# Block products for the second token pair, late gate tiles and one-column modulation products in an adaLN attention and gMLP block

## The chip, the cores and the metric

One core of a Trainium2 chip runs the whole kernel. The time is the device time of one launch in microseconds (us), the median of several runs of the same program. A profiled execution has its own time; its span, from the first to the last instruction that the profile shows, is a little shorter.

## What is computed

One batch of 2048 tokens of width 512 goes through two residual blocks that are modulated by a condition c: linear attention with 32 heads, then a gated MLP whose gate mixes along the tokens.

```python
mod = (silu(c) @ w_mod).reshape(1, 6, 1, -1)
sa, ca, ga, sb, cb, gb = (mod[:, i] for i in range(6))
h = layernorm(x) * (1 + ca) + sa
x = x + ga * linear_attention(h, wqkv, wo)      # phi = elu + 1, 32 heads of 16
h = layernorm(x) * (1 + cb) + sb
z = gelu(h @ w_in)                              # [2048, 1376]
z1, z2 = z[..., :688], layernorm(z[..., 688:])
g = w_sp @ z2 + b_sp[:, None]                   # [2048, 2048] x [2048, 688]
out = x + gb * ((z1 * g) @ w_out)
```

All of it is float32.

## The kernel before, in words

**Numbers.** TensorE takes operands of type float32r here, so every factor is kept in two parts, a high part (`x_hi`, made by ACT as a copy into float32r) and a low part (`x - x_hi`, made by DVE or POOL), and every product is three matmuls: high by high, high by low, low by high. "A low part" of a tile is thus one subtraction of its size on DVE or POOL, behind a copy on ACT.

**Phases.** The tokens are 16 tiles of 128. Phase 1 (to some 200 us) reads the modulation, folds `1 + ca` into the attention's weights, normalizes, and forms keys, values and their sums. At the start `col_mm` (L189) multiplies blocks of `w_mod` by a repeated column of silu(c); the result is a 128 by 4 by 128 PSUM tile, all columns of a block alike, which `mean_col` (L324) copies as it stands and `col_end` (L204) reads one column of. Dummy products (`du`, on the tile `warm`) fill PE's first microseconds.

Phase 2 goes tile by tile through the attention's output, `h2`, its transposed parts `ht2`, and `z_mm` (L652): 24 matmuls of 128x344 each for z1 (`z0` in the order) and z2 (`z1` in the order). `z1_out` puts gelu(z1) into DRAM (`z1d`). `z2_out` makes `zz`, which is normalized (`zb` is the shift), parked in DRAM (`zd`), and split into `z2` (`zh` high part on ACT, `zo` low part on POOL, L695).

Phase 3 is the spatial mix `w_sp · z2`. The 16 row tiles are 8 pairs, and the two halves of z2's width are 344 columns each. A row tile by plain products is four chains `pp` t,k of 24 matmuls, eight such chains for a pair. Pairs 2 to 7 use seven block products (as in Strassen's scheme over token pair and width half): `pr` p,h,k is product k over half h of the 8 pairs of source tiles, 12 matmuls, 14 of them for a pair. They need block sums of `w_sp` (`ss` by DVE, split by `fh` and `fl`: tiles `f`, `sa`), and differences of z2 tiles: `ts` j loads two parked tiles back (`e`, `o`, L868), `td` j makes four differences on DVE (L873 to L876), `th` and `tl` j,k split them (tiles `t4` to `t6`, and parts of z2; L896 on DVE). `cs`, `cd`, `ce` add the products into U; `um` multiplies by z1, read back by `lz`; `up`, `ux`, `ug` transpose U (planes of 16 bits, DMA transpose, merge), `uq` parks it. Then `wm` multiplies by `w_out`, and `ot` stores.

Before, pair 0 is all plain. Pair 1 is mixed: four of its eight plain chains, `pp` 2,2 2,3 3,2 3,3, are added into the same PSUM banks as products k = 1, 2, 3, 4 and a bank 0 (table `MIX`, L939), the rest comes from seven products over half h = 0 alone, and one more addition stands at L979.

**What sets the order.** The program is written in one line of time: `ORDER` (L796) for phases 1 and 2 and `ORDER3` (L1096) for phase 3 are lists of the operations above. Each engine executes its instructions in that order and waits at the first one whose input or buffer isn't ready; SP issues all DMAs in that order as well. `SLOTS` (L53) assigns each tile of a kind to a buffer, one digit per tile, so a digit decides whose readers a new tile waits for. The pool `tq` (tiles e, o, t) is laid over the space of phase 2's pools `ws`, `ta` and `tb`, which are closed by then.

Of the kernel before, what the change touches and what calls it, by code (L numbers as in the profile page):

```python
# [26 lines left out]
def block_kernel(ctx: ExitStack, tc: tile.TileContext, x, x_t, w_qkv, w_o, w_in, w_sp, b_sp, w_out,  # L27
# [3 lines left out]
    def pool(name, bufs, space=None, stack=None):  # L31
        if space is None:
# [156 lines left out]
    def col_mm(m, kc):  # L189
        if m not in CP:  # L190
            CP[m] = ps("t", [P, KC, P], f"pcol{m}")
        for i in range(KC):
            n = NCOL[m] = NCOL.get(m, 0) + 1
            mm(CP[m][:, i], RAW["mod", m, kc // 2][:, kc % 2, i * P:(i + 1) * P],
               sil[:, kc:kc + 1].to_broadcast([P, P]), start=n == 1, stop=n == KC * KC, skip_group_check=True)
# [482 lines left out]
    def z2_norm(t):  # L678
        z = ZZ[t]
        b = sm([P, 1], "zb")  # L680
        nc.vector.scalar_tensor_tensor(b, MEAN["z", t], -1.0, RSTD["z", t], op0=OP.mult, op1=OP.mult)
# [12 lines left out]
    def z2_lo(t):  # L694
        nc.gpsimd.tensor_sub(Z2[t][:, 1], ZZ[t], f(Z2[t][:, 0]))  # L695
# [84 lines left out]
    def hx_lo(t):  # L780
# [16 lines left out]
        lm1,0 lm1,1 si du1 du2 du3 du4 cm1,0 lm1,2 cm1,1 cm1,2 lm1,3 cm1,3 mc lw1,0 du5 mr1,0 mr1,1 ly1 th1  # L797
        tl1 ce1 lw1,1 mr1,2 mr1,3 ly0 th0 tl0 ly2 th2 wf1,3 qh1,3 qg1,3 lw0,0 tl2 lw0,1 wf1,1 mr0,0 mr0,1
# [29 lines left out]
        zh1 zo1 zp1 hl6 zl7 z08 hp9 x110 am12 g18 lX12 ah12 z16 hm9 hh9 g26 h210 hp10 hl9 z09 l5 zl6 d214 ap14
        g19 hm10 lX14 hh10 zn6 hl10 z19 zo0 g29 al12 am13 ah13 al13 am14 ah14 al14 x111 zh5 zn7 lX13 z06 g16
        h211 ap15 zp7 zo5 z18 g28 zh7 zo7 zl9 wo12 x112 h212 hp11 hm11 hh11 zn9 z010 g110 wo13 zp4 z110 zh4  # L830
        hp12 x113 am15 ah15 lh0,0 al15 g210 zp6 hl11 z011 wo15 h213 hp13 hm12 hh12 hl12 zo4 aH0,0 zl8 zn8 zh8
        z012 g112 wo14 hm13 zp8 x115 aL0,0 zh9 g111 h215 hp15 zl10 z111 hh13 g211 hl13 zn10 zh10 zp3 x114 h214
        zh6 lh1,0 zp9 zo9 z112 zp10 z113 hm15 zo8 g212 hp14 aH1,0 aL1,0 hh15 hl15 g213 zl11 z013 g113 zo3 z015
        hm14 hh14 hl14 g115 z114 g214 zn11 zp11 zh11 mV5,0 mV5,1 mS5 z014 mB5 g114 z115 g215 zo10 zo6
# [132 lines left out]
    def c_sum(p, k):  # L967
# [42 lines left out]
    def u_merge(t):  # L1010
        merge(UC[t][1], UC[t][0].rearrange("p a b -> p (a b)").rearrange("p (a b) -> p a b", b=2))
# [170 lines left out]
```

## Time and profile before

| What | us |
|---|---|
| median of 3 runs | 620.29 |
| fastest and slowest of them | 619.77, 621.38 |
| profiled execution, its own time | 620.6 |
| its span | 618.8 |
| PE busy in the span | 613.3 |
| DVE busy | 487.0 |
| ACT busy | 336.1 |
| POOL busy | 224.0 |
| mean granted TensorE clock | 0.999 of full speed |

How to read the rows that follow: a row of a timeline has the start in us from the beginning of the span, the busy time, the engine, the line of the kernel, the operation with output and inputs, the shapes, and how many of the same stand behind one another; in brackets the idle time ahead of it and what ended it. A row of groups has the busy sum, the mean in ns of one, and the idle time ahead of the group's instructions. PE is TensorE, DVE VectorE, ACT ScalarE, POOL GpSimd, and SP issues the DMAs. Starts of neighbouring matmuls overlap by their pipeline, so a cadence is taken from start to start. The time with no PE work at the end is the last addition and store (from 615.7 to 618.8).

### The profile page before, as it was taken

Reading aid. Unit: us, or ns where it says so; the run is one execution under the profiler, and the core shown is the slowest. Engines: PE = TensorE matmul, PEld = TensorE weight load, DVE = VectorE, ACT = ScalarE, POOL = GpSimd, SP = SyncE. Lnnn points to the kernel's source line nnn. Section 1 sums busy time; section 2 is a strip of 40 time slices with the busy share of each in tenths; the row PEclk is TensorE's granted clock in tenths of the full one; section 3 lists DMA queues with packets and bytes.
Section 4 is the critical chain, followed back from the end, with each engine's and each line's share of the span. In section 5 each row is a group of like instructions: output and inputs, shape, how many; then the busy total and the mean of one; then the engine's idle time right before and its main releaser. Section 6 shows DMA issues by size and latency. Waiting matters only on the chain.

```text
span 618.8 us, 9545 instructions
## 1 busy us (share of the span) xinstructions
PE 613.3 (99%) x3387; PEld 560.3 (91%) x3387; DVE 487.0 (79%) x902; ACT 336.1 (54%) x580; POOL 224.0 (36%) x185
## 2 busy tenths in 40 slices
PE   9999999999999999999999999999999999999997
PEld 6788888888899999999999999999999999998886
DVE  2999889897788878787786799997767787887661
ACT  2876767565656667565536464454354453544320
POOL 0843444637666576464252420132112111300000
PEclk9999999999999999999999999999999999999999
DMA  8463323261244667566844965552496555989962
GB/s 297 162 191 118 105 68 103 83 194 37 64 122 120 163 175 190 169 199 176 201 138 161 355 217 132 203 168 73 155 199 211 154 182 145 287 267 253 295 223 81
DMA packets 91022, 105.74 MB, mean 171 GB/s; under 512 B 57088, under 2 KB 57600, under 8 KB 90976
## 3 DMA queue, kind: packets, MB, share of 16 engines
q1 hardware_dynamic: 90976, 105.15, 57.2%
q8 instruction: 26, 0.43, 0.3%
q14 instruction: 20, 0.16, 0.1%
HBM read 66.07 MB, written 25.95 MB: 149 GB/s over the span
## 4 chain that ended last, share of the span: by engine, by line
PE 69%; DVE 14%; DMA 7%; issue 5%; POOL 2%; ACT 2%; SPq 1%; POOLq 0%; DVEq 0%; ACTq 0%
PE z L659 15%; PE P L937 13%; PE pout L111 3%; PE pout L112 3%; PE pout L110 3%; DMA raw_wsp<-in_w_sp 3%; PE g L110 2%; PE g L112 2%; PE qp L112 2%; PE qp L111 2%; PE qp L110 2%; PE g L111 2%; PE kp L110 2%; PE po L112 2%; PE kp L111 2%
## 5 line engine op out<-in xcount | busy, mean ns | idle before, releaser
L659 PE MATMUL z<-win,ht 128*128 128x344 f32 x768 | 123.0, 320 | 0.2 <-DVE ht L298 0.2
L659 PEld LDWEIGHTS z<-win,ht 128*128 128x128 f32 x768 | 121.4, 188 | 1.2 <-DVE ht L298 0.5
L937 PE MATMUL P<-z,f 128*128 128x344 f32 x624 | 103.3, 320 | 0.4 <-DVE f L927 0.4
L937 PEld LDWEIGHTS P<-z,f 128*128 128x128 f32 x624 | 99.1, 188 | 0.9 <-DVE f L927 0.7
L927 POOL TENSOR_TENSOR f<-raw_wsp,f 128x512 fp32r<-128x512 f32 x26 | 37.9, 1467 | 138.4 <-ACT f L924 132.1
L254 POOL TENSOR_TENSOR mv<-ve,mhalf 128x1 f32<-128x1 f32 x48 | 35.4, 740 | 54.9 <-DVE ve L253 52.5
L924 ACT ACTIVATE f<-raw_wsp 128x512 fp32r<-128x512 f32 x52 | 31.8, 626 | 29.9 <-PE P L937 14.1
L924 ACT ACTIVATE f<-sa 128x512 fp32r<-128x512 f32 x39 | 24.2, 629 | 33.2 <-DVE sa L914 10.1
L477 POOL TENSOR_TENSOR pksum<-pksum,tk 128x512 f32<-128x512 f32 x15 | 23.1, 1538 | 41.4 <-DVE tk L449 34.2
L927 DVE TENSOR_TENSOR f<-sa,f 128x512 fp32r<-128x512 f32 x39 | 28.5, 741 | 9.6 <-ACT f L924 9.6
L111 PE MATMUL pout<-wout,ut 128*128 128x512 f32 (+1 forms) x85 | 32.2, 379 | 0.2 <-DVE wout L1063 0.2
L110 PE MATMUL pout<-wout,ut 128*128 128x512 f32 (+1 forms) x85 | 32.2, 379 | 0.0
L112 PE MATMUL pout<-wout,ut 128*128 128x512 f32 (+1 forms) x85 | 32.2, 379 | 0.0
L695 POOL TENSOR_TENSOR z<-zz,z 128x688 fp32r<-128x688 f32 x16 | 29.2, 1842 | 7.5 <-ACT z L692 7.5
L937 PE MATMUL Pq<-z,wsp 128*128 128x344 f32 x192 | 30.8, 321 | 0.0
L937 PEld LDWEIGHTS Pq<-z,wsp 128*128 128x128 f32 x192 | 30.6, 188 | 0.0
L1032 ACT ACTIVATE ut<-ur 128x384 fp32r<-128x384 f32 x32 | 15.2, 518 | 24.8 <-DMA ur<-ud 15.8
L268 ACT COPY uca<-us 128x768 uint16<-128x768 uint16 x32 | 25.0, 828 | 5.3 <-PE P L937 3.6
L588 POOL TENSOR_TENSOR prod<-pq,zrep 128x512 f32<-128x512 f32 x16 | 21.7, 1370 | 14.5 <-ACT zrep L714 4.2
L110 PE MATMUL po<-m,pt 128*128 128x512 f32 x64 | 25.3, 396 | 0.0
L112 PE MATMUL po<-m,pt 128*128 128x512 f32 x64 | 25.3, 396 | 0.0
L110 PE MATMUL g<-pkhl,hhl 128*128 128x512 f32 x64 | 25.3, 395 | 0.0
(260 smaller groups left out, 1557.8 us busy)
## 6 DMA issues: line engine op xcount, KB each, us to landing
raw_wsp<-in_w_sp SPq DMA_DIRECT2D x32, 512.0 KB, 4.7
ud<-uca SPq DMA_DIRECT2D x16, 384.0 KB, 3.3
ur<-ud SPq DMA_DIRECT2D x16, 384.0 KB, 4.2
z1d<-z SPq DMA_DIRECT2D x16, 344.0 KB, 2.3
zd<-zz SPq DMA_DIRECT2D x16, 344.0 KB, 2.7
z1r<-z1d SPq DMA_DIRECT2D x16, 344.0 KB, 4.1
xt<-in_x_t SPq DMA_DIRECT2D x16, 256.0 KB, 3.0
x<-in_x SPq DMA_DIRECT2D x16, 256.0 KB, 2.9
```

The lines of the kernel that those rows point to most:

```text
L110: mm(o, a_hi, b_hi, start=first, stop=False, **kw)
L111: mm(o, a_hi, b_lo, start=False, stop=False, **kw)
L112: mm(o, a_lo, b_hi, start=False, stop=last, **kw)
L254: nc.gpsimd.tensor_tensor(mv[:, 1:2], ve, mhalf, op=OP.pow)
L268: nc.scalar.copy(pl[:, h], v[:, :, h])
L477: nc.gpsimd.tensor_add(pksum, pksum, PK[t])
L588: nc.gpsimd.tensor_mul(pr, PQ[t], KV["z"])
L659: mm(p[:, b, :HB], a[:, i, kc], win[h][:, j, kc, b * HB:(b + 1) * HB], start=kc == 0 and k == 0, stop=kc == KC - 1 and k == 2)
L695: nc.gpsimd.tensor_sub(Z2[t][:, 1], ZZ[t], f(Z2[t][:, 0]))
L924: nc.scalar.activation(SF[p, h, k][:, 0], s_src(p, h, k), AF.Copy)
L927: eng.tensor_sub(SF[p, h, k][:, 1], s_src(p, h, k), f(SF[p, h, k][:, 0]))
L937: mm(B[key][:, :HB], a[:, x_], b[:, y_], start=i == 1, stop=i == n)
```

## The change

What it does, by part:

1. `col_mm` multiplies by one column of silu(c) instead of a column repeated 128 times, into a 128 by 4 tile. `mean_col` lets ACT repeat each column as it copies. One more step of dummies, `du6`, stands in the order behind `du5`.
2. Pair 1 is treated like pairs 2 to 7: 14 products of 12 matmuls. `MIX` and the addition at L979 are gone; the plain chains of pair 0 use banks 4 to 7.
3. z1 of tiles 12 to 15 moves behind phase 2: `zw` is its 24 matmuls in two of the banks 0 to 3 (by the tile's parity), `zg` its two gelus of 344 on ACT and its store.
4. The low part of z2 goes to DVE for tiles 11 to 15.
5. `zb` is made by a `tensor_scalar` of two operations, not by a `scalar_tensor_tensor`.
6. The merge of U's planes is copied by ACT, not by DVE.
7. From early in phase 2 on, `ORDER`, `ORDER3` and the slots are new. Everything ahead of some 210 us stands as before, save item 1.

```diff
     def col_mm(m, kc):
         if m not in CP:
-            CP[m] = ps("t", [P, KC, P], f"pcol{m}")
+            CP[m] = ps("t", [P, KC], f"pcol{m}")
         for i in range(KC):
             n = NCOL[m] = NCOL.get(m, 0) + 1
-            mm(CP[m][:, i], RAW["mod", m, kc // 2][:, kc % 2, i * P:(i + 1) * P],
-               sil[:, kc:kc + 1].to_broadcast([P, P]), start=n == 1, stop=n == KC * KC, skip_group_check=True)
+            mm(CP[m][:, i:i + 1], RAW["mod", m, kc // 2][:, kc % 2, i * P:(i + 1) * P],
+               sil[:, kc:kc + 1], start=n == 1, stop=n == KC * KC, skip_group_check=True)
...
-        nc.scalar.activation(WC["c"], CP[1], AF.Copy, scale=1.0 / D, bias=1.0 / D)
+        nc.scalar.activation(WC["c"], CP[1][:, :, None].to_broadcast([P, KC, P]), AF.Copy, scale=1.0 / D, bias=1.0 / D)
...
-        nc.vector.scalar_tensor_tensor(b, MEAN["z", t], -1.0, RSTD["z", t], op0=OP.mult, op1=OP.mult)
+        nc.vector.tensor_scalar(b, MEAN["z", t], RSTD["z", t], -1.0, op0=OP.mult, op1=OP.mult)
...
-        nc.gpsimd.tensor_sub(Z2[t][:, 1], ZZ[t], f(Z2[t][:, 0]))
+        (nc.gpsimd if t < 11 else nc.vector).tensor_sub(Z2[t][:, 1], ZZ[t], f(Z2[t][:, 0]))
...
+    def z_late(t):
+        ZB[t, 0] = [bank(2 * (t % 2) + b, f"z0{b}_{t}") for b in range(2)]
+        a = HT2[t]
+        for kc in range(KC):
+            for k, (i, j) in enumerate(((0, 0), (0, 1), (1, 0))):
+                for b in range(2):
+                    mm(ZB[t, 0][b][:, :HB], a[:, i, kc], win[0][:, j, kc, b * HB:(b + 1) * HB],
+                       start=kc == 0 and k == 0, stop=kc == KC - 1 and k == 2)
+
+    def z1_late(t):
+        z = sb("st", [P, 2, HB], F32, f"z1_{t}")
+        for b, p in enumerate(ZB.pop((t, 0))):
+            nc.scalar.activation(z[:, b], p[:, :HB], AF.Gelu_apprx_tanh)
+        Z1D[t] = dram.tile([P, FH], F32, tag=f"z1d{t}", name=f"z1d{t}")
+        dma(Z1D[t], z.rearrange("p a b -> p (a b)"))
...
-    MIX = {(2, 0): ((1, 2), 4, 36), (2, 1): ((1, 3), 5, 36), (3, 0): ((1, 4), 6, 36), (3, 1): ((1, 0), 7, 24)}
-
     def prod(p, h, k):
-        n = 24 if p > 1 else 36 if k in (2, 3, 4) else 12
         for j in range(4):
-            chain((p, k), BANK[k], n, SF[p, h, k][:, :, j], t_of(4 * h + j, k))
+            chain((p, k), BANK[k], 24, SF[p, h, k][:, :, j], t_of(4 * h + j, k))
...
-                key, where, n = (("q", t, h), 2 * t + h, 3 * NT) if t < QUAD else MIX[t, h]
-                chain(key, where, n, WSP[t, k][:, :, s], Z2[4 * k + s][:, :, h * HB:(h + 1) * HB])
+                chain(("q", t, h), 4 + 2 * t + h, 3 * NT, WSP[t, k][:, :, s], Z2[4 * k + s][:, :, h * HB:(h + 1) * HB])
...
-            if p == 1:
-                nc.vector.tensor_add(U[t1][:, HI], B[p, 0][:, :HB], U[t1][:, HI])
...
-        merge(UC[t][1], UC[t][0].rearrange("p a b -> p (a b)").rearrange("p (a b) -> p a b", b=2))
+        merge(UC[t][1], UC[t][0].rearrange("p a b -> p (a b)").rearrange("p (a b) -> p a b", b=2), nc.scalar.copy)
...
     ORDER3 = """
-        zl14 aH0,1 pp1,0 lh2,1 zl12 zn12 aH1,1 zo11 zl13 zn13 lh0,1 zp13 zp12 zl15 aH2,2 aL0,1 aH0,2 zn15 zp15
+        lh0,1 zw13 aH0,2 zl12 zn12 lh2,0 zw12 zl14 zn14 zl13 zp12 zp14 aH0,1 lh1,1 aL0,1 pp0,1 aH1,1 zn13 zh13
...
```

**DVE at the first difference.** These are DVE's instructions before the change, at the step from phase 2 to phase 3, up to the first difference of z2 tiles (`e3`, `o3`). `wsp` are low parts of the plain chains' weights, the numbers at the ends tell tiles of one name apart.

```order
L757 TENSOR_TENSOR wsp2_2_3835<-raw_wsp_2_1_3794,wsp2_2_3835 128x512
L757 TENSOR_TENSOR wsp0_2_3838<-raw_wsp_0_1_3821,wsp0_2_3838 128x512
L757 TENSOR_TENSOR wsp1_1_3807<-raw_wsp_1_0_3448,wsp1_1_3807 128x512
L681 SCALAR_TENSOR_TENSOR zb_3909<-mv2_3761 128x1
L757 TENSOR_TENSOR wsp1_3_3916<-raw_wsp_1_1_3850,wsp1_3_3916 128x512
L873 TENSOR_TENSOR e3_3998<-e3_3998 128x344
L874 TENSOR_TENSOR e3_3998<-o3_3999,e3_3998 128x344
```

And these stand there after it, up to the same difference.

```order
L698 TENSOR_TENSOR z2_14_3819<-zz_14_3539,z2_14_3819 128x688
L760 TENSOR_TENSOR wsp1_3_3822<-raw_wsp_1_1_3738,wsp1_3_3822 128x512
L760 TENSOR_TENSOR wsp1_2_3825<-raw_wsp_1_1_3738,wsp1_2_3825 128x512
L698 TENSOR_TENSOR z2_11_3528<-zz_11_3421,z2_11_3528 128x688
L698 TENSOR_TENSOR z2_15_3857<-zz_15_3582,z2_15_3857 128x688
L698 TENSOR_TENSOR z2_13_3772<-zz_13_3532,z2_13_3772 128x688
L698 TENSOR_TENSOR z2_12_3854<-zz_12_3454,z2_12_3854 128x688
L892 TENSOR_TENSOR e3_3890<-e3_3890 128x344
L893 TENSOR_TENSOR e3_3890<-o3_3891,e3_3890 128x344
L894 TENSOR_TENSOR o3_3891<-o3_3891,e3_3890 128x344
L895 TENSOR_TENSOR o3_3891<-o3_3891 128x344
L760 TENSOR_TENSOR wsp0_3_3903<-raw_wsp_0_1_3644,wsp0_3_3903 128x512
```

The low parts of five z2 tiles, which POOL made, now stand ahead of the first difference on DVE, and the low part of wsp0_3 stands behind it.

**SP at the first loads.** These are the DMAs that SP issues around the first loads of `e` and `o`, after the change; `z1d` are stores of late z1 tiles, `zd` of parked tiles.

```order
L691 DMA zd15_3817<-zz_15_3582 128x688
L691 DMA zd13_3888<-zz_13_3532 128x688
L887 DMA e3_3890<-zd6_3357 128x688
L887 DMA o3_3891<-zd7_3091 128x688
L880 DMA z1d13_3901<-z1_13_3898 128x688
L887 DMA e2_3932<-zd4_2960 128x688
```

Before, the same place reads:

```order
L688 DMA zd15_3843<-zz_15_3696 128x688
L142 DMA raw_wsp_1_1_3850<-in_w_sp 128x1024
L688 DMA zd14_3968<-zz_14_3619 128x688
L868 DMA e3_3998<-zd6_3249 128x688
L868 DMA o3_3999<-zd7_3077 128x688
L868 DMA e2_4011<-zd4_3197 128x688
```

The load of e3 stands behind the stores of the parked tiles in both. A store of z1 of tile 13 now stands between the first two pairs of loads.

More of the change, by code (lines that the diff above doesn't have):

```diff
@@ L828, in block_kernel @@
[L828 to L832, printed above, removed]
@@ L835, in block_kernel @@
+        x114 zo9 hm12 hh12 z011 g111 aH1,0 hl12 hm13 hh13 zp6 h214 wo15 x115 hp14 h215 zh8 aL1,0 z111 hl13
+        g211 hm14 hp15 z112 g212 zn10 zl11 hh14 z113 hl14 z114 zh10 zo10 zp8 zn11 zh11 zp11 g213 hm15 hh15
+        hl15 g214 z115 lh0,0 aH0,0 aL0,0 zp10 mS5 mB5 g215 zo6 zo8
     """
@@ new lines, in block_kernel @@
+        zl15 aL1,1 pp1,1 zg12 zn15 zp15 zh14 zo14 aH1,3 aL1,3 aH1,2 aL1,2 zw15 zh12 zo11 zh15 zo15 zw14 zo13
+        zo12 zp13 ts3 td3 zg13 aH0,3 th3,6 aL0,3 pp0,3 ts2 td2 th3,7 th2,7 tl2,7 th2,4 aL0,2 pp0,2 fh1,0,2
+        fg1,0,2 ts0 tl2,4 td0 ts6 td6 th6,5 lh3,0 th0,4 ts1 ss1,0,3 ss1,0,1 ss1,0,2 zg14 tl0,4 tl6,5 th3,5
+        pp1,3 td1 zg15 fh1,0,6 fl1,0,6 tl3,7 th1,5 tl1,5 ss1,0,4 th1,4 tl1,4 th6,7 tl6,7 fh1,0,1 ts5 lz0 td5
+        pp1,0 ts4 td4 th5,4 tl5,4 fh1,0,3 th2,6 pp0,0 th4,5 tl4,5 fl1,0,3 tl3,5 ce0,0 th1,7 th6,4 tl1,7
@@ new lines, in block_kernel @@
+        fl1,0,1 th0,6 tl0,6 pp1,2 th4,7 th5,6 tl5,6 tl3,6 th1,6 tl1,6 fh1,0,5 tl2,6 th4,6 pr1,0,6 tl4,7
+        fl1,0,5 pr1,0,1 th0,7 ce0,1 th3,4 tl3,4 lh3,1 lh2,1 ss1,1,3 fh1,1,1 fl1,1,1 th0,5 tl0,5 th2,5 tl2,5
+        fh1,1,7 fl1,1,7 fh1,1,2 tl6,4 fg1,1,2 pr1,0,3 um0 lz1 ce1,0 ce1,1 th6,6 tl6,6 ss1,1,1 pr1,0,5 pr1,1,2
+        ss1,1,2 fh1,0,7 fl1,0,7 th5,7 lh4,1 fh1,0,4 fg1,0,4 ts7 up0 ux0 pr1,0,2 tl5,7 td7 th7,5 th7,7 tl7,7
+        lh4,0 pr1,1,1 fh1,1,5 pr1,0,4 lh5,1 fh1,1,4 fg1,1,4 tl7,5 tl0,7 fl1,1,5 cs1,1 cd1,2 pr1,1,7 fh1,1,6
```

137 lines of the change are left out of this document (67 added, 70 removed).

## The prediction

> **What bounds the kernel now.** I read the busy shares first, then the chain that ended last, then the rows of PE, DVE, SP and the DMA queues around the start of the block products, since from there on nothing stands where it stood.
>
> ```profile
> PE 613.3 (99%) x3387; PEld 560.3 (91%) x3387; DVE 487.0 (79%) x902; ACT 336.1 (54%) x580; POOL 224.0 (36%) x185
> PE 69%; DVE 14%; DMA 7%; issue 5%; POOL 2%; ACT 2%; SPq 1%; POOLq 0%; DVEq 0%; ACTq 0%
> ...
> 345.00:385.00 40.00, 40.00 (x254) 40.00 (x253) 39.20 (x70) 19.53 (x42) 7.74 (x5) 1.00 0.71 233
> ```
>
> PE is busy for 99% of the span, so a matmul that goes is worth its cadence and only a hole on PE can cost. The third row is the window from 345 to 385 us (sum; PE, PE's weight load, DVE, ACT, POOL busy; granted clock 1.00; DMA share; GB/s). In these 40 us DVE is busy for 39.2: here a second engine has almost no room, and what the change does to DVE here decides.
>
> **The products that go.** The rows of PE from the last work of phase 2 to the first product that needs a tile of differences:
>
> ```profile
> 329.57 3.94 PE L659 MATMUL z<-win,ht 128*128 128x344 f32 x24
> 333.35 7.75 PE L937 MATMUL Pq<-z,wsp 128*128 128x344 f32 x48
> ...
> 344.74 23.08 PE L937 MATMUL Pq<-z,wsp 128*128 128x344 f32 x144
> 367.65 2.05 PE L937 MATMUL P<-z,f 128*128 128x344 f32 x12
> 369.54 7.77 PE L937 MATMUL P<-z,wsp 128*128 128x344 f32 x48
> ...
> 379.04 0.64 PE L937 MATMUL P<-t_0r,f 128*128 128x344 f32 x3
> ```
>
> From start to start, 12 matmuls of 128x344 take 1.89 us (367.65 to 369.54) and 144 take 22.91, 0.158 us each; the 24 of a z tile take 3.78 (329.57 to 333.35). Pair 1 had 96 plain and 84 block matmuls, 180; it now has 7 products by 2 halves by 12, 168. Twelve go: 12 x 0.158 = **-1.9 us**. The z1 products of tiles 12 to 15 (4 x 3.78) only move.
>
> **The start.**
>
> ```profile
> 0.98 3.78 PE L172 MATMUL warm<-ones 128*128 128x128 f32 x16 [0.98 <-POOL tiny L124]
> 4.81 4.94 PE L194 MATMUL pcol<-sil,raw_mod 128*128 128x128 f32 x32
> 14.38 3.67 PE L332 MATMUL wm<-raw_qkv,cbr 128*128 128x512 f32 x8 [0.24 <-DMA raw_qkv<-in_w_qkv]
> 23.47 1.05 PE L201 MATMUL pcol<-ones,yp 128*128 128x1 f32 x8
> ```
>
> The 32 matmuls of L194 include the 16 that shrink; one takes 4.94/32 = 0.154 us, while a one-column matmul of L201 takes 1.05/8 = 0.131. With all 32 counted the saving is 0.7 us at most. But the product at 14.38 was released by the DMA of raw_qkv, which doesn't move, and the added dummies (du6) stand ahead of that same wait. So I take **0**, with -0.7 as the other end.
>
> **The new wait.** Let T be the end of z2's product of tile 15 on PE, the last work of phase 2. Before, T = 333.35, and the first product of t tiles starts at 379.04, T + 45.7. After, T comes about 15.1 us earlier on the clock, because four z1 tiles of 3.78 stand behind it now. PE then has two small products for a column (mB5, some 0.47, three cadences, an estimate), the four late z1 (15.1) and eight plain chains at some 3.8 (30.4): it comes to pr1,0,6 at T + 46.0, and wants t6_0r then, t6_1r at T + 46.5 and t6_2r at T + 46.95. PE's demand is where it was. DVE's supply is not.
>
> ```profile
> 343.10 0.38 SPq L868 DMA_DIRECT2D e<-zd  x1
> 343.53 0.45 SPq L868 DMA_DIRECT2D o<-zd  x1
> ...
> 346.79 1.98 DVE L873 TENSOR_TENSOR e<-e 128x344 f32<-128x344 f32 x1
> 348.80 0.52 DVE L874 TENSOR_TENSOR e<-o,e 128x344 f32<-128x344 f32 x1
> 350.94 0.51 DVE L873 TENSOR_TENSOR e<-e 128x344 f32<-128x344 f32 x1
> ...
> 353.02 0.69 DVE L757 TENSOR_TENSOR wsp<-raw_wsp,wsp 128x512 fp32r<-128x512 f32 x1
> 353.62 0.51 DVE L873 TENSOR_TENSOR e<-e 128x344 f32<-128x344 f32 x1
> ...
> 358.85 0.52 DVE L896 TENSOR_TENSOR t_0r<-o,t_0r 128x344 fp32r<-128x344 f32 x1
> 359.28 0.51 DVE L896 TENSOR_TENSOR t_3r<-e,t_3r 128x344 fp32r<-128x344 f32 x1
> ...
> 376.87 0.51 DVE L896 TENSOR_TENSOR t_1r<-o,t_1r 128x344 fp32r<-128x344 f32 x1
> ```
>
> Before, SP issued the loads e3, o3 at T + 9.75, DVE's first difference (td3) started at T + 13.4, and the last low part ahead of PE's need ended at 377.4, 1.7 us early. DVE was already the tighter engine.
>
> ```profile
> L695 POOL TENSOR_TENSOR z<-zz,z 128x688 fp32r<-128x688 f32 x16 | 29.2, 1842 | 7.5 <-ACT z L692 7.5
> L692 ACT ACTIVATE z<-zz 128x688 fp32r<-128x688 f32 x16 | 12.0, 770 | 0.2
> L754 ACT ACTIVATE wsp<-raw_wsp 128x512 fp32r<-128x512 f32 x12 | 7.2, 620 | 1.4 <-DMA raw_wsp<-in_w_sp 1.4
> L997 DVE TENSOR_TENSOR us<-us,z1r 128x688 f32<-128x688 f32 x14 | 12.7, 906 | 2.2 <-DMA z1r<-z1d 2.0
> ...
> e<-zd SPq DMA_DIRECT2D x8, 344.0 KB, 4.1
> o<-zd SPq DMA_DIRECT2D x8, 344.0 KB, 4.9
> zd<-zz SPq DMA_DIRECT2D x5, 344.0 KB, 2.4
> ```
>
> After, the order on each engine gives this chain. ACT's wsp1_2 reuses a buffer that the plain chain pp0,1 reads, which ends at T + 0.47 + 7.56 + 3.8 = T + 11.8. Behind it on ACT stand wsp1_2 (0.62) and the high parts of z2_12 and z2_15 (0.77 each): T + 14.0. The low parts of z2_15, z2_13 and z2_12 are DVE's now; DVE never did one, so they are bounded by POOL's 1.84 above and the 128x344 cadence twice (0.9) below, and I take 0.85 to 0.9, the 128x688 row of L997: T + 16.6. The loads e3 and o3 take over buffers that zz_12 lay in, so SP issues e3 only then, T + 17.0, and o3 0.43 behind, as in the rows above. DVE's next instruction is td3: while it waits, all that stands behind it (six more td, every low part of a t tile, pair 1's block sums and low parts, wsp0_3 for the chain pp0,3) waits as well. With a landing of 4.5, the mean of the two rows, o3 is there at T + 21.9; the three remaining operations of td3 at 0.55 end at T + 23.55.
>
> Behind them DVE has 48 instructions to the end of t6_0r: 6 td of 2.08 (350.94 to 353.02) = 12.5, 9 of 128x512 at 0.60 (353.02 to 353.62) to 0.69, 5.6, 13 low parts at 0.43 (358.85 to 359.28), 5.6, and U's first part 0.5; 24.2 in all, and three low parts more to t6_1r, 25.5. That is T + 49.1 against PE's need at T + 46.5: **+2.6 us**. Ends: with a landing of 2.4, the nearest faster row of that size, +0.5; with 4.9 and DVE at the pace of the dense stretch of before (the row of 1.98 has 1.5 us over the 0.52 of its like; one and a half such, an estimate, are 2.2 more), +5.2. I keep 0.5 to 5.2.
>
> The Trainium skill, "DMA: Bandwidth & Descriptors", section "Anatomy of one DMA — SWDGE (gpsimd) path", fits a transfer as about 2.0 us and the bytes at 436 GB/s; an estimate by it is 2.8 us for 344 KB, and the wait would be 0.9 instead of 2.6. These loads go through SP's queue and the rows say 4.1 and 4.9, so I stay with the rows.
>
> **The rest.**
>
> ```profile
> L278 DVE COPY uca<-ucb 128x768 uint16<-128x768 uint16 x32 | 18.4, 631 | 3.7 <-DMA ucb<-uca 3.5
> L268 ACT COPY uca<-us 128x768 uint16<-128x768 uint16 x32 | 25.0, 828 | 5.3 <-PE P L937 3.6
> L681 DVE SCALAR_TENSOR_TENSOR zb<-mv 128x1 f32<-128x1 f32 x16 | 7.6, 473 | 2.6 <-POOL mv L254 2.6
> L253 DVE TENSOR_SCALAR ve<-mv 128x1 f32<-128x1 f32 x48 | 7.4, 154 | 1.7
> ...
> 394.15 0.48 PE L937 MATMUL P<-t_0r,f 128*128 128x344 f32 x2
> 394.83 0.43 PE L937 MATMUL P<-t_0r,f 128*128 128x344 f32 x1 [0.20 <-DVE f L927]
> ...
> 440.77 1.74 PE L937 MATMUL P<-z,f 128*128 128x344 f32 x10
> 442.89 1.37 PE L937 MATMUL P<-z,f 128*128 128x344 f32 x7 [0.38 <-DVE f L927]
> ...
> 554.41 0.39 PE L110 MATMUL pout<-wout,ut 128*128 128x512 f32 x1
> 554.99 0.50 PE L111 MATMUL pout<-wout,ut 128*128 128x512 f32 x1 [0.19 <-DVE wout L1063]
> ```
>
> The merge copies leave DVE, 32 x 0.631 = 20.2 us by the mean, for ACT at 32 x 0.828 = 26.5; the zb change takes 16 x (0.473 - 0.154) = 5.1 off DVE, and the five low parts put 4.5 on it. ACT was 54% busy and PE covers it; if that cover failed, a late merge would hold up u's transfer, which is needed only for the output products. What DVE gains pays only in PE's holes. There are three with DVE as releaser: 394.83 less 394.15 less two cadences, 0.36; 442.89 less 440.77 less ten, 0.54; 554.99 less 554.41 less 0.23, 0.35. Together 1.25. A new order meets its own deadlines in other places; I take -0.5, between -1.25 (all gone, none new) and +0.75 (as many new and 0.75 beyond).
>
> **Sum.** -1.9 + 0 + 2.6 - 0.5 = +0.2 on the profiled execution's 620.6 (span 618.8 and 1.8 around it): 620.8. That execution lies 0.3 over the median of the runs, 620.29, so the forecast is **620.5 us**.
>
> **The rivals.**
>
> A: the wait doesn't arise. If e3 and o3 are issued a little earlier than I chain them and land in 2.4 us, td3 ends by T + 21 and PE finds every tile. What is left is -1.9 and up to -1.25 at the holes, with up to -0.7 at the start: 616.4 to 618.4. For it: PE's demand and DVE's work between are the same size as before, and 1 us of chain either way settles it. Against it: both landing rows, and SP's own order.
>
> B, slower: DVE bounds pair 1 throughout. The window row has 0.8 us of DVE's time to spare in 40. If the operations under contention stretch as the 1.98 us one did, PE waits not once but at pr1,0,6 and again for the t5 and t4 tiles and the td7 that stand behind: 5.2 - 1.9 - 0.5 = +2.8, 623.1. It decides from a wait of 4.3 us in all. Against it: behind pr1,0,6 the merges that stood on DVE are gone.
>
> C: one hole of more than about 3 us also slows what follows. The first 16 dummies take 3.78/16 = 0.236 us each and the products behind them 0.154, so a start from rest costs 16 x 0.08 = 1.3 us here; on top of a wait of 3.5 or more that gives 622.4 and over. The Trainium skill, "TensorE: Matmul & The Clock Gate", section "What's actually happening", says that an idle window of some 3.4 us halves the clock. No run here shows it after the start: the granted clock is 1.00 and no later hole is over 0.6 us. The low parts come 0.43 apart, so my wait would be cut in pieces, which speaks against C.
>
> **How the numbers follow.** Forecast 0.43; A 0.32; B 0.21; C 0.04. A measurement of this kernel can tell about 0.3% from no change: faster is below 618.4, slower above 622.2. Some of A ends at the border and so does some of the forecast: faster 0.33, same 0.44, slower 0.23. The range takes in most of A, down to 616.9, and B up to 623.1, and leaves out a tenth on each side.
>
> **What would show it.** PE's count on the page should go from 3387 to 3377: twelve products fewer, two dummies more. Right: a hole in front of, or within, the first L956 product with t6 tiles, released by DVE L915, while DVE's wait ahead of its first L892 is released by the DMA of e or o. Wrong for A's reason: no hole there, and e3 issued well under 17 us behind the last z2 product. Wrong for B's: holes with releaser L915 or L946 at several products of pair 1. If the start is worth something, the product of raw_qkv begins ahead of 14.38. What would make the forecast wrong altogether is a hole in phase 2, where z1 and z2 tiles now come in another order and whose handovers I took as covered.

## The result: 628.66 us, 1.2% slower, and the profile after

The changed kernel takes 628.66 us in the median of four runs (624.73 to 630.44), the kernel before beside it 620.33. The ratio is 1.012 with a 95% interval from 1.0095 to 1.0144, that is 5.9 to 8.9 us more. The forecast was 620.5, within 616.9 to 623.1: wrong, on the slower side. The profiled execution has a span of 627.0 us, 8.2 more than the 618.8 of before.

The page of the changed kernel has eight matmuls fewer on PE, but more time. (The prediction had ten fewer; the added `du6` is four passes, not two.)

```profile
PE 619.2 (99%) x3379; PEld 563.4 (90%) x3379; DVE 475.7 (76%) x881; ACT 365.1 (58%) x619; POOL 216.8 (35%) x180
```

PE is busy 5.9 us longer with less to do. So a part of the loss is no waiting at all: matmuls took longer. The timeline of PE at the start of the changed kernel shows the first of it.

```profile
4.72 6.96 PE L197 MATMUL pcol<-sil,raw_mod 128*128 128x1 f32 x32
11.54 2.06 PE L175 MATMUL warm<-ones 128*128 128x128 f32 x8
13.38 9.02 PE L335 MATMUL wm<-raw_qkv,cbr 128*128 128x512 f32 x16
28.29 1.05 PE L204 MATMUL pcol<-ones,yp 128*128 128x1 f32 x8 [0.19 <-POOL yp L229]
```

The one-column products take 6.96 us where the 128-column ones took 4.94. The eight products of L204 start at 28.29; the same ones (L201) started at 23.47 before. The start is **4.8 us** late, and the rest of phase 2 stays late with it. The window view counts what PE did in equal stretches; first the kernel before, columns as in the prediction.

```profile
4.80:7.00 2.20, 2.19 (x10) 2.20 (x11) 0.00 (x0) 0.00 (x0) 0.00 (x0) 1.00 0.98 336
7.30:9.50 2.20, 2.20 (x22) 2.20 (x22) 0.00 (x0) 0.00 (x0) 0.00 (x0) 1.00 0.94 348
```

Then the same stretches of the changed kernel, and two of the products on raw_qkv:

```profile
4.80:7.00 2.20, 2.20 (x11) 2.20 (x12) 0.00 (x0) 0.00 (x0) 0.00 (x0) 1.00 0.94 276
7.30:9.50 2.20, 2.20 (x12) 2.20 (x12) 0.00 (x0) 0.00 (x0) 0.00 (x0) 1.00 0.95 315
13.40:17.40 4.00, 4.00 (x6) 1.67 (x6) 0.75 (x2) 0.66 (x2) 0.00 (x0) 1.00 1.04 405
17.60:21.60 4.00, 4.00 (x11) 1.82 (x10) 2.59 (x5) 1.18 (x2) 1.10 (x1) 1.00 0.68 251
```

Before, PE's pace doubles inside the modulation products, near 7 us: 10 of them in 2.2 us, then 22. After, it stays at 11 or 12, with one column as with 128. The pace doubles only near 17.5, inside the products on raw_qkv (6 in 4 us, then 11). PE is busy all the time in these rows, and the column of the granted clock says 1.00 in all of them: here the clock is read from the count, not from that column.

The second loss is at the end of phase 2, on PE's timeline of the changed kernel:

```profile
322.50 0.40 PE L240 MATMUL pmod<-yh,ones 128*128 128x512 f32 x1
322.99 0.50 PE L241 MATMUL pmod<-yl,ones 128*128 128x512 f32 x1
323.33 0.32 PE L872 MATMUL z<-win,ht 128*128 128x344 f32 x1
324.18 7.67 PE L872 MATMUL z<-win,ht 128*128 128x344 f32 x47 [0.53 <-ACT mod L243]
331.69 7.77 PE L956 MATMUL Pq<-z,wsp 128*128 128x344 f32 x48
```

T, the end of the last z2 product, is 322.50. The second matmul of the late z1 waits for ACT's read of the modulation's bank: from 322.50 to 331.69 are 9.19 us where two small products and 48 matmuls need 8.0. **1.1 us**.

The third is where the prediction had its main term. SP and DVE first, then PE, in the changed kernel:

```profile
340.32 0.32 SPq L887 DMA_DIRECT2D e<-zd  x1
...
343.27 0.52 DVE L892 TENSOR_TENSOR e<-e 128x344 f32<-128x344 f32 x1 [3.08 <-issue]
344.47 0.52 DVE L893 TENSOR_TENSOR e<-o,e 128x344 f32<-128x344 f32 x1 [0.68 <-DMA o<-zd]
...
371.77 0.52 DVE L915 TENSOR_TENSOR t_0r<-o,t_0r 128x344 fp32r<-128x344 f32 x1
```

```profile
365.75 4.15 PE L956 MATMUL Pq<-z,wsp 128*128 128x344 f32 x25
370.91 0.42 PE L956 MATMUL P<-t_0r,f 128*128 128x344 f32 x1 [1.01 <-ACT t_0r L911]
372.34 0.94 PE L956 MATMUL P<-t_0r,f 128*128 128x344 f32 x2 [1.01 <-DVE t_0r L915]
373.08 1.49 PE L956 MATMUL P<-t_1r,f 128*128 128x344 f32 x3
374.36 1.06 PE L956 MATMUL P<-t_2r,f 128*128 128x344 f32 x3
375.22 0.89 PE L956 MATMUL P<-t_3r,f 128*128 128x344 f32 x3
375.95 3.94 PE L956 MATMUL P<-z,f 128*128 128x344 f32 x24
```

PE comes to pair 1's first product at 369.73 (one cadence behind the last of the plain ones) and is done with it at 375.95: 6.2 us for twelve matmuls that need 1.9, **4.3 us**. Two holes of 1.0 are waits; but the matmuls on t_2r, 0.29 apart (0.86 for three), run at half the pace. Here the granted clock shows it, in windows of the same execution:

```profile
370.00:372.00 2.00, 0.42 (x1) 0.19 (x1) 2.00 (x6) 1.36 (x3) 0.00 (x0) 1.00 0.00 0
372.00:374.00 2.00, 1.60 (x4) 1.17 (x5) 2.00 (x6) 1.68 (x5) 0.00 (x0) 0.59 0.00 0
374.00:376.00 2.00, 2.00 (x9) 2.00 (x9) 2.00 (x5) 1.75 (x5) 0.00 (x0) 0.56 0.00 0
```

The ledger by the two traces: +4.8 at the start, +1.1 at the late z1, +4.3 at pair 1, -1.9 for the twelve products, -0.9 for two holes of before that are gone (0.36 and 0.54), and +0.7 for a new hole near 495, released by DVE: 8.1 of the 8.2 us. The kernel's other row that I had mis-sized is the merge on ACT:

```profile
L281 ACT COPY uca<-ucb 128x768 uint16<-128x768 uint16 x32 | 31.9, 1065 | 12.8 <-DMA ucb<-uca 12.8
```

1.065 us each where I took 0.828 from ACT's copies of the same size in the other direction.

### The profile page after: what moved, and what is told of

Read it like the earlier page. It is cut to its first block, busy times and chain, and to the rows that moved or that the text cites. A ratio compares the mean times of both kernels' runs of the same rounds, so it can differ in the third digit from the quotient of the medians.

```text
span 627.0 us, 9536 instructions
## 1 busy us (share of the span) xinstructions
PE 619.2 (99%) x3379; PEld 563.4 (90%) x3379; DVE 475.7 (76%) x881; ACT 365.1 (58%) x619; POOL 216.8 (35%) x180
## 5 line engine op out<-in xcount | busy, mean ns | idle before, releaser
L956 PE MATMUL P<-z,f 128*128 128x344 f32 x672 | 110.9, 320 | 0.4 <-DVE us L980 0.4
L662 PE MATMUL z<-win,ht 128*128 128x344 f32 x672 | 107.6, 320 | 0.2 <-DVE ht L301 0.2
L956 PEld LDWEIGHTS P<-z,f 128*128 128x128 f32 x672 | 106.6, 188 | 0.8 <-DVE us L980 0.7
L662 PEld LDWEIGHTS z<-win,ht 128*128 128x128 f32 x672 | 106.2, 188 | 1.1 <-DVE ht L301 0.4
L946 POOL TENSOR_TENSOR f<-raw_wsp,f 128x512 fp32r<-128x512 f32 x28 | 42.3, 1520 | 172.9 <-ACT f L943 163.4
L946 DVE TENSOR_TENSOR f<-sa,f 128x512 fp32r<-128x512 f32 x42 | 33.8, 815 | 19.8 <-ACT f L943 19.8
L943 ACT ACTIVATE f<-sa 128x512 fp32r<-128x512 f32 x42 | 26.1, 629 | 26.9 <-DVE sa L933 9.6
L943 ACT ACTIVATE f<-raw_wsp 128x512 fp32r<-128x512 f32 x56 | 34.1, 626 | 12.5 <-PE P L956 7.3
L281 ACT COPY uca<-ucb 128x768 uint16<-128x768 uint16 x32 | 31.9, 1065 | 12.8 <-DMA ucb<-uca 12.8
L1098 DVE TENSOR_TENSOR x<-x,pout 128x512 f32<-128x512 f32 (+1 forms) x17 | 10.9, 655 | 19.1 <-PE pout L1094 19.0
```

The source lines that it names most:

```text
L281: copy(o[:, :, h], plt[:, h * n:(h + 1) * n].rearrange("p a b -> p (a b)"))
L662: mm(p[:, b, :HB], a[:, i, kc], win[h][:, j, kc, b * HB:(b + 1) * HB], start=kc == 0 and k == 0, stop=kc == KC - 1 and k == 2)
L943: nc.scalar.activation(SF[p, h, k][:, 0], s_src(p, h, k), AF.Copy)
L946: eng.tensor_sub(SF[p, h, k][:, 1], s_src(p, h, k), f(SF[p, h, k][:, 0]))
L956: mm(B[key][:, :HB], a[:, x_], b[:, y_], start=i == 1, stop=i == n)
```

## The experiments

Each kernel is the changed kernel or the one before with the edit shown. All of them are timed beside the kernel before. "Start" is when the eight small products of L201 or L204 begin (23.47 before), in the profiled execution.

| Kernel | median, us | before beside it | ratio, 95% interval | start |
|---|---|---|---|---|
| changed | 628.66 | 620.33 | 1.012, 1.0095 to 1.0144 | 28.29 |
| a_wide | 625.83 | 621.03 | 1.0065, 1.0042 to 1.0087 | 23.78 |
| b_col | 624.05 | 621.03 | 1.0046, 1.0027 to 1.0064 | 27.59 |
| a_zo | 626.88 | 621.03 | 1.0089, 1.0067 to 1.0110 | 28.73 |
| a_pad | 626.49 | 621.03 | 1.0086, 1.0063 to 1.0108 | 25.64 |
| b_warm | 625.33 | 621.10 | 1.0075, 1.0045 to 1.0104 | 27.66 |
| b_mix | 630.78 | 621.10 | 1.0125, 1.0082 to 1.0167 | 33.50 |
| a_best | 626.69 | 621.10 | 1.0087, 1.0067 to 1.0107 | 24.13 |
| a_merge | 636.28 | 621.10 | 1.0249, 1.0226 to 1.0272 | 26.05 |
| a_again | 627.21 | 621.08 | 1.0098, 1.0078 to 1.0117 | 28.04 |
| a_ord | 625.98 | 621.08 | 1.0082, 1.0062 to 1.0102 | 24.20 |
| a_best2 | 623.27 | 621.08 | 1.0033, 1.0019 to 1.0047 | 23.59 |
| a_best3 | 627.30 | 620.80 | 1.0112, 1.0091 to 1.0133 | 23.98 |
| a_best4 | 623.71 | 620.44 | 1.0050, 1.0036 to 1.0065 | 24.02 |

With one-column products the start lies anywhere from 24.2 to 28.7 (leaving out b_mix) in executions of nearly the same code; with 128-column products it is 23.5 to 24.1. The traces show what differs. The dummies end near 4.7. With 128-column products the pace doubled in all six traces, at some moment from 3.8, still in the dummies, to 7.1 (a matmul from 0.21 us to 0.11). With one-column products behind the same 16 dummies it doubled by 5.5 in three traces (a_pad, a_merge, a_ord), and not before 16.4 in four (changed, a_again, a_zo, b_col). In the three it fell again, 3.3 to 4.1 us after the one-column products had begun; a_pad:

```profile
5.00:8.00 3.00, 3.00 (x28) 2.98 (x27) 0.00 (x0) 0.00 (x0) 0.00 (x0) 1.00 0.90 276
8.50:11.50 3.00, 3.00 (x12) 2.48 (x13) 0.00 (x0) 1.09 (x2) 0.00 (x0) 0.50 1.03 397
```

So the one-column start costs more or less by whether the clock has risen before the narrow work takes over, and that changes from one execution to the next. It also spreads the times of the changed kernel.

### The start

**a_wide** puts the 128-column products back.

```diff
-            mm(CP[m][:, i:i + 1], RAW[...], sil[:, kc:kc + 1], ...)
+            mm(CP[m][:, i], RAW[...], sil[:, kc:kc + 1].to_broadcast([P, P]), ...)
-... lw1,0 du5 du6 mr1,0
+... lw1,0 du5 mr1,0
```

> The changed kernel with the 128-column products of the kernel before at the start (and without du6). Theory G (one-column products don't keep PE's clock up, so they run at the cold cadence of 0.213 us, and so do the dummies and the first products behind them): the start falls back by all of the 4.8 us that it lost, the pcol products come to 4.9 us, the second block of kp starts at 24.4 again, 628.7 - 4.8 = 623.9 us. Rival D (the start is late by the two added dummies and by a transfer): the product on raw_qkv is still late and no more than 1.0 us comes back, 627.7.

The start came back: L204 began at 23.78. The ratio is 1.0065, for 1.012 of the changed kernel and 1.0098 of it in a second measurement (a_again below): 2.0 to 3.4 us, less than the 4.5 of the start, and the time is 1.9 over the expectation. PE, being earlier, met two new waits: 1.1 us for DVE's wsp0_3 near 343, which stands behind the first difference in DVE's queue, and 0.9 for a block of f by POOL near 447. In pair 1's first product its holes of 0.45, 1.0 and 0.3 were followed by 3.4 us at a granted clock of 0.50.

**b_col** makes the one edit alone, on the kernel before.

```diff
-            mm(CP[m][:, i], RAW[...], sil[:, kc:kc + 1].to_broadcast([P, P]), ...)
+            mm(CP[m][:, i:i + 1], RAW[...], sil[:, kc:kc + 1], ...)
-        nc.scalar.activation(WC["c"], CP[1], AF.Copy, ...)
+        nc.scalar.activation(WC["c"], CP[1][:, :, None].to_broadcast([P, KC, P]), AF.Copy, ...)
```

> The kernel before with only the one-column products and the repeating copy (no du6). Theory G: the start loses 4 to 5 us by itself, 624.3 to 625.3 us, with products behind raw_qkv at 0.85 us a piece until the clock rises. Rival N (they are cheaper or hidden, as I had it before the run): 619.6 to 620.3.

3.0 us slower by the medians (1.7 to 4.0 by the interval), and 4.1 late at the start of the trace:

```profile
12.96 8.74 PE L332 MATMUL wm<-raw_qkv,cbr 128*128 128x512 f32 x16
21.13 6.28 PE L417 MATMUL kp<-wk,ht 128*128 128x512 f32 x24
27.59 1.05 PE L201 MATMUL pcol<-ones,yp 128*128 128x1 f32 x8 [0.17 <-POOL yp L226]
```

The 16 products on raw_qkv run without a wait from 12.96 to 21.13, where the trace of before had waited for the transfer until 14.38. The edit alone costs this, and my **0** for the start falls. The added dummy step of the changed kernel isn't in it. The start came as late as theory G had it, the time 0.25 us under its range. Of the ten executions five have a mean granted clock of 0.994 to 0.997 and took 622.0 to 624.1 us; the other five have 0.999 or 1.000 and took 624.0 to 626.6. That fits a clock that rose early in the first five and fell again, as in a_pad, but only one of the ten has a trace.

**b_warm** and **b_mix** give PE full-width work again, ahead of the one-column products or between them.

```diff
-... du4 cm1,0 lm1,2 cm1,1 cm1,2 lm1,3 cm1,3 mc
+... du4 du11 du12 du13 du14 cm1,0 lm1,2 cm1,1 cm1,2 lm1,3 cm1,3 mc            # b_warm
+... du4 cm1,0 du11 du12 lm1,2 cm1,1 du13 du14 cm1,2 du15 du16 lm1,3 cm1,3 du17 mc   # b_mix
```

> The kernel before with one-column products, and 16 more matmuls of dummies (128 columns) ahead of them. Theory G1 (the clock rises only under full-width work and falls again under one-column work): the clock rises while the dummies run (near 7.1 us, as before), the 32 one-column products run at about 0.112 us, and then the clock is low again in the products behind raw_qkv: the start stays 2 us or more late, kp's second block at 26.5 or later, 622.5 us or more. Theory G2 (it only has to be raised once): the start is level with that of before, kp's second block at 24.4 to 24.9, 620.3 to 621.

> The kernel before with one-column products and 28 matmuls of dummies (128 columns) put between them and behind them. G1: full-width work in between raises the clock and keeps it, kp's second block at 24.4 to 25.5, 620.3 to 621.5. G2 and the theory that one-column products are slow by themselves: as late as with one-column products alone, 28.5, 624.

The windows of b_warm show the clock rise and fall:

```profile
7.30:9.50 2.20, 2.20 (x23) 2.20 (x21) 0.00 (x0) 0.00 (x0) 0.00 (x0) 1.00 0.83 318
9.50:11.50 2.00, 2.00 (x14) 2.00 (x14) 0.00 (x0) 0.00 (x0) 0.00 (x0) 0.66 1.04 413
12.60:17.00 4.40, 4.40 (x7) 1.82 (x7) 1.29 (x2) 1.47 (x4) 0.00 (x0) 0.50 1.03 405
```

Behind the dummies the pace is 23 in 2.2 us; after some three us of one-column products (they begin at 7.39) it is 14 in 2.0 with a granted clock of 0.66, and the products on raw_qkv run at 0.50. That is theory G1: a one-column product keeps PE busy in the profile but doesn't keep the clock up. b_mix went against both expectations: in its trace, with half the matmuls at full width, the clock didn't rise before the products on raw_qkv, the start came 10.0 us late (33.50), and the time was 1.0125 of before. Of the 10.0 us the 28 added matmuls themselves are 6.0, at 0.213 each. So wide work in equal parts in between wasn't enough there; how much would be was not tried, and one of the four executions, without a trace, took only 624.70.

### Pair 1

**a_zo** moves one instruction on DVE.

```diff
-... zh12 zo11 zh15 zo15 zw14 zo13 zo12 zp13 ts3 td3
+... zh12 zo11 zo12 zh15 zw14 zo13 zo15 zp13 ts3 td3
```

> The changed kernel with DVE's low part of z2_12 ahead of those of z2_13 and z2_15, nothing else. Theory O (SP's e3 waits for that one low part, and all of DVE's differences wait for e3): e3 is issued about 1.6 us earlier (338.7 instead of 340.3 on the trace's clock), DVE's whole queue to the t6 tiles moves up as much, the gap in pair 1's first product shrinks from 3.3 to 1.7 us and with it part of the slow clock behind it: 1.6 to 2.6 us faster, 626.1 to 627.1. Rival Q (DVE's throughput, not where it starts): the gap stays, 628.7.

```profile
339.25 0.32 SPq L887 DMA_DIRECT2D e<-zd  x1
...
371.53 0.58 PE L956 MATMUL P<-t_0r,f 128*128 128x344 f32 x2 [0.91 <-DVE t_0r L915]
372.81 0.58 PE L956 MATMUL P<-t_1r,f 128*128 128x344 f32 x2 [0.33 <-DVE t_1r L915]
```

Counted from its own last z2 product (T was 322.96 here) the load e3 went out at T + 16.3, 1.5 us earlier, and pair 1's first product ended 3.9 us after PE came to it, not 6.2; behind the shorter holes the matmuls run at full pace. That is theory O in the trace. The ratio of 1.0089 against the changed kernel's 1.012, or 1.0098 when it was timed again below, has overlapping intervals, so the time alone doesn't decide it.

**a_pad** fills the hole.

```diff
+    def pad(n):
+        p = bank(2, "pad")
+        for _ in range(n):
+            mm(p[:, :HB], ones, Z2[0][:, 0, :HB], start=True, stop=True)
-... th4,6 pr1,0,6
+... th4,6 pd22 pr1,0,6
```

> The changed kernel with 22 spare products of 128x344 (3.5 us at full clock) on a free PSUM bank ahead of pair 1's first product, so that PE isn't idle there; nothing of the result depends on them. Theory K (a hole of 2 us there also lowers PE's clock for some 3 us): the product behind them runs at 0.158 a matmul instead of 0.29, it ends at 375.1 instead of 375.95, and the kernel is 0.8 to 1.0 us faster, 627.8, although PE has more to do. Rival W (the matmuls are slow because each waits for its tile): nothing comes back, 628.7 or a little more.

```profile
368.76 3.68 PE L965 MATMUL pad<-z,ones 128*128 128x344 f32 x22
372.27 0.63 PE L956 MATMUL P<-t_0r,f 128*128 128x344 f32 x3
374.15 3.94 PE L956 MATMUL P<-z,f 128*128 128x344 f32 x24
```

From PE's arrival to the end of the product are 5.4 us with 22 matmuls more, 6.2 without them. The product itself takes 1.88 us at full pace. So without the hole the pace is whole, and the slow clock had cost 0.8 to 1.0. This is one execution, and holes don't always bring the slow clock: in a_again they were 0.7, 1.0 and 0.3, and the pace stayed whole. All traces together say a little more. Behind the start, the granted clock fell to 0.5 in five places, each right behind holes: 1.0 and 1.0 in the changed kernel, 0.45, 1.0 and 0.3 in a_wide, 0.7 and 0.9 in a_best, 2.95 in a_merge, 4.1 in a_best3. It stayed up behind those of a_again, behind a single hole of 2.3 in a_merge, and behind one of 1.5 in a_pad near 346. So a slow clock came only behind holes, and the size of the hole alone doesn't say whether it comes. (The kernel's time fell by 2 us, but its start was 2.6 earlier, since the clock rose early in this execution; so the time says nothing on this.)

**a_merge** puts the merge back on DVE.

```diff
-        merge(UC[t][1], ..., nc.scalar.copy)
+        merge(UC[t][1], ...)
```

> The changed kernel with the merge of U's planes on DVE again. My step (the merge costs nothing on either engine): 628.7 within 0.6. Rival (on ACT it is on the way, since a copy that waits for its transposed planes holds up the c copies behind it): the hole of 0.5 near 494 goes, and 0.5 to 1.5 us come back.

Both expectations failed: it is 8 us slower than the changed kernel.

```profile
417.77 1.07 DVE L281 COPY uca<-ucb 128x768 uint16<-128x768 uint16 x2 [5.39 <-DMA ucb<-uca]
418.73 0.68 DVE L946 TENSOR_TENSOR f<-sa,f 128x512 fp32r<-128x512 f32 x1
...
419.46 1.83 PE L956 MATMUL P<-z,f 128*128 128x344 f32 x10 [2.33 <-DVE f L946]
```

DVE stands 5.4 us at the merge for the transposed planes, and the low part of f behind it is what PE waits for. PE's four waits for low parts of f by DVE come to 6.4 us (2.3 here, 2.95 near 483, 0.7 and 0.4). It isn't the merge's 1 us but its wait that matters. On ACT the same waits are 12.8 us over all 32 merges of the changed kernel (the row above), and no hole of PE of 0.4 us or more is put down to them there.

**a_best**, **a_ord**, **a_best2**, **a_best3** and **a_best4** mend the order around the first differences, step by step.

```diff
# all of them: zo12 as in a_zo, wsp0_3 ahead of the first difference, td4 behind the t6 low parts,
# and in SLOTS the digits of tq in the new order
-... ts3 td3 zg13 aH0,3 th3,6 aL0,3 pp0,3
+... ts3 zg13 aH0,3 aL0,3 td3 th3,6 pp0,3          # a_best: ts3 aH0,3 aL0,3 td3 zg13
-... ts4 td4 th5,4 ... tl0,6 pp1,2 th4,7 th5,6 tl5,6 tl3,6 th1,6 tl1,6 fh1,0,5 tl2,6
+... ts4 th5,4 ... tl0,6 pp1,2 th1,6 tl3,6 tl2,6 tl1,6 td4 th4,5 tl4,5 th4,7 th5,6 tl5,6 fh1,0,5
# a_best: mS5 mB5 ahead of the last z2 product; a_ord, a_best2 to 4: banks laid in order instead
+    for k in range(8):
+        bank(k, f"lay{k}")
# a_ord: one-column products; the others 128-column
# a_best3: ce0,1 lz1 ahead of td4; a_best4: ce0,1 alone
```

> The changed kernel with 128-column products at the start, the low part of z2_12 ahead of z2_13 and z2_15, wsp0_3 ahead of the first difference, td4 and what hangs on it behind the t6 low parts, and the broadcast of mod 5 ahead of the last z2 product. Theory O with G: start back to 24.4 to 24.6; no hole at the late z1 products (it was 1.0); no hole at the plain chain that needs wsp0_3; the gap in pair 1's first product 0.7 us or less and no slow clock behind it. From 628.7: -4.5 -1.0 -3.7 = 619.5 us, 0.998 of before. Rival Q (DVE is the bound in pair 1): the gap only moves to later products of pair 1, 3 us come back there, 622.5.

a_best lost what it won by two moves of mine: the modulation's split was late at its new place (0.7 for yl and 0.9 for ht behind it), and the gelus of late tile 13, put behind wsp0_3 on ACT, kept PE from the next late z1 for 1.1 us. Behind the first two of these holes the clock fell to half from 317 to 321, and 1.2 us went at a block of f by POOL near 448. Pair 1's first product itself had no hole. The time was 7 us over theory O's. Of the next three runs the first is the changed kernel again, and the other two leave both moves out.

> The changed kernel as it is, once more, so that it is timed on the same chip and beside the same runs of before as the next two. 1.012 of before within 0.3%; the start 2 to 5 us late by how long the clock is low, and the gap in pair 1's first product 2.5 us or more.

> The changed kernel with only its order around the first differences mended (low part of z2_12 first; the two gelus of late tile 13 and wsp0_3 ahead of the first difference; td4 and what hangs on it behind the t6 low parts) and the PSUM banks laid in their numbers' order, so that the first late z1 doesn't take the bank that mod 5 is read from. One-column products stay. Theory O: no gap in pair 1's first product (3.3 of waiting and 1.0 of slow clock less) and none at the late z1 (1.0 less), 0.4 to 0.9 new behind it: 4 us faster than the changed kernel as it is. Rival Q: what is won comes back within pair 1, 1 us or less.

> The same order, and 128-column products at the start. G and O together: 3 to 4.5 us faster than that order with one-column products; less what the hole at the fourth pair takes back, where POOL's f waits for ACT's merges and their DMA (1.3 with the early start in two runs). 622 us or a little over, 1.002 of before.

The late z1 has no hole in either mended kernel. In pair 1 the hole got smaller but moved on; PE in a_best2:

```profile
364.98 0.58 PE L958 MATMUL P<-t_0r,f 128*128 128x344 f32 x2 [0.57 <-DVE t_0r L917]
370.71 2.19 PE L958 MATMUL P<-z,f 128*128 128x344 f32 x12 [1.04 <-DVE us L982]
```

a_ord is 1.2 us under a_again by the medians, with overlapping intervals: near Q's 1 us or less, far from O's 4. (Its trace is of its fastest execution, 622.72 against 624.6 to 626.7 for the others, and there the clock had risen early; so its start of 24.20 isn't that of its median.) a_best2 is 2.7 us under a_ord, and here the intervals are apart: that is the start, in a pair of kernels that differ only in it (and in `du6`). Its expectation of 622 was 1.3 too low.

> The mended order with 128-column products (the last run's kernel), and ce0,1 (DVE's read of pair 0's second bank) and the load lz1 ahead of td4, since the 1.0 us hole behind pair 1's first product was released by ce0,1 in the last two runs. If it is the order of DVE's queue: that hole goes and nothing of 0.5 us or more comes in its place, 1.0 us faster, 622.2 us, 1.002 of before. If it is DVE's throughput (rival Q): the product behind it waits for a low part or a block of f as long, and the time stays at 1.003.

> As the last run, but ce0,1 alone stands ahead of td4; the load lz1 is back behind the loads of w_sp, since SP waited there for ce0,1 and the w_sp blocks behind it came late (DVE waited 3.2 us for raw_wsp). If pair 1's holes are the order of the queues: no hole of 1.0 behind pair 1's first product and none of 4 at its third t product, 622.2 us, 1.002 of before, about 1 us better than the order before it. If DVE's throughput bounds: 623.3, and the missing 1.0 us stands at the next products of pair 1.

In a_best3 the hole of 1.04 went, but I had moved the load lz1 as well. SP stood at it, the blocks of w_sp behind it came late, and PE waited once for 4.1 us. That was my error in the edit. a_best4 moves ce0,1 alone:

```profile
367.12 3.93 PE L958 MATMUL P<-z,f 128*128 128x344 f32 x24
371.37 0.43 PE L958 MATMUL P<-t_0r,f 128*128 128x344 f32 x1 [0.32 <-ACT t_0r L913]
372.65 0.58 PE L958 MATMUL P<-t_0r,f 128*128 128x344 f32 x2 [0.85 <-DVE t_0r L917]
```

The second and third product run through (24 in 3.9 us), and the hole stands in the fourth, 0.3 and 0.85. The time is 1.005, no better than a_best2 and nearer to the expectation for a full DVE. A window of a_best4 and the same of the changed kernel have DVE nearly full in this stretch:

```profile
365.00:380.00 15.00, 13.49 (x83) 12.73 (x82) 14.54 (x28) 9.49 (x20) 2.87 (x2) 1.00 0.37 111
...
365.00:380.00 15.00, 12.92 (x69) 11.96 (x68) 14.83 (x34) 10.46 (x24) 2.20 (x1) 0.89 0.32 117
```

DVE is busy 14.5 and 14.8 of 15 us. Each place that I mended gave its hole to the next thing that DVE owes. So in pair 1 DVE has no room to catch up. But at the head of its work for pair 1 DVE stood and waited for the loads of e and o, in the mended orders too; a_best2:

```profile
335.84 0.52 DVE L894 TENSOR_TENSOR e<-e 128x344 f32<-128x344 f32 x1 [0.64 <-DMA e<-zd]
338.57 0.52 DVE L895 TENSOR_TENSOR e<-o,e 128x344 f32<-128x344 f32 x1 [2.21 <-DMA o<-zd]
341.51 0.52 DVE L894 TENSOR_TENSOR e<-e 128x344 f32<-128x344 f32 x1 [1.33 <-DMA e<-zd]
342.44 0.52 DVE L895 TENSOR_TENSOR e<-o,e 128x344 f32<-128x344 f32 x1 [0.41 <-DMA o<-zd]
```

These are 4.6 us (3.6 in a_best4), more than PE's holes in pair 1 (2.2 in a_best2, 1.5 in a_best4). So what PE waits for is DVE's work behind a late start. That an earlier start helps is seen in a_zo. But no run shortened the loads themselves or took work off DVE, so how much of the holes belongs to each stays open. No kernel here beats the one before; a_best2, at 1.0033, comes closest.

## Why the prediction was wrong

**The start** is the step that failed, the term that I sized "0, with -0.7 as the other end". It is +4.8 in the trace (0.7 to 5.3 in the other traces with one-column products, b_mix left out), and b_col shows the edit alone at +3.0 in time. The working error: I divided a group's time by its count (4.94/32 = 0.154; all 32 shrink, not 16) though the group has two paces in it, 0.21 and 0.11, and set that against 0.131 of a one-column product from a part of the program where the clock was up. The rows to see it were there: the 16 dummies at 0.236 stand right ahead of it, and I used them for rival C only. With the clock low a one-column product costs as much as a wide one, and a stretch of them leaves the clock low for what comes behind, past the transfer that I counted on as cover.

**The products that go**: -1.9, as worked out.

**The new wait**: the chain was right link by link, and the hole came where I had put it, in the first product with t6 tiles, with ACT's high part of t6_0r ahead of the releaser that I had named, DVE's L915. Its size was 2.6 where 4.3 came. SP issued e3 at T + 17.8 (I had 17.0), o3 was used at T + 22.0 (21.9). From there to the end of t6_0r I had 25.9 us (1.65 and 24.2); DVE took 27.8, to T + 49.8, since it waited 0.8 for the next pair of loads and one difference took 1.6 instead of 0.5. PE came 1.2 later too, by the late z1. So the waits were 3.3, inside the 0.5 to 5.2 that I gave, and 1.0 is the clock, which the sum didn't have. In a_again, without the slow clock, the whole was 3.0.

**Rival C**, at 0.04, had this mechanism and a wrong condition: I asked for one hole of over 3 us, and it came behind two of 1.0 with one matmul between them. The rule that I named beside it, of the Trainium skill ("TensorE: Matmul & The Clock Gate", section "What's actually happening"), speaks of an idle window of some 3.4 us; the trace has the clock at 0.59 behind 2.0 us of holes within some 2.6, while in a_merge it stayed up behind one hole of 2.3.

**Rival B**, at 0.21, did not come by its own sign: I asked for holes at several products of pair 1, and in the changed kernel they stand in the first alone. The mended orders bring the holes at later products, with DVE full there. Of B's mechanism, operations stretched by contention, the changed kernel shows one: 1.1 of DVE's 1.9 us over my sum, the 0.8 of waits being the rest.

**The late z1** I had at its bare 3.78: 1.1 more, for a PSUM bank whose reader I didn't look up.

**The rest**: the two holes at 394 and 442 did go, and 0.7 came at 495, so -0.2 net, within -1.25 to +0.75. The merge I called free on either engine. On DVE it would cost 8 us in this order. On ACT no hole of the changed kernel is put down to it; but in four kernels with the early start (a_wide, a_best, a_best2, a_best4) PE has 0.6 to 1.2 us at a block of f by POOL near 445, and some 8 us ahead of each ACT, whose high part of f POOL needs, stands 3.5 to 4.1 us at a merge. That the merges cause these holes is likely and not shown.

## What to carry to other kernels

Before a product is made narrower, look at the pace of PE around it by counting matmuls in short windows: a mean over a group can hide a change of clock, and here narrow work left the clock down for the wide work behind it. When an order is moved, add up the busy time of every engine in the stretch that PE then waits for; if one has no room, look at when its work can start as well: here mending one place in its order only handed the hole to the next. An instruction that waits for a DMA belongs on the engine whose queue can best stand still; here that was ACT and not DVE.

## What the runs showed of the hardware that was not expected

Matmuls of 128x128 and of 128x1 were 0.21 us apart at the low clock and 0.11 at the high one: the width made no difference.

With work of 128 columns from the first dummy on (at 0.98) the clock rose 2.8 to 6.1 us later, at no fixed moment, and stayed up through the start. Where one-column products took over at 4.6 to 4.8, it either had risen by 5.5 or waited for wide work: 16.4 to 17.4, which is 4.4 to 5.9 us after the first wide dummy behind them. Under one-column products alone a risen clock fell within 2.8 to 4.1 us (b_warm, a_pad, a_merge, a_ord), though PE was busy without a pause in three of the four.

Later the clock fell only behind holes of PE, the least of them 1.6 us in two pieces (a_best), but not behind all: one of 2.3 (a_merge) and three of 2.0 in all (a_again) left it up.

The granted clock's column read 1.00 in the first 17 us of the changed kernel though the pace was half.
